# Crossbar transposes, a new decay path and regrouped gates in a fused gate-loop and GEGLU kernel

## The chip, the cores and the metric

The kernel runs on one core of one Trainium2 chip. The metric is device microseconds (us) of that core, the median of several executions. Before the change: 344.27 us, median of 3 runs (342.91 to 344.88). Ratios and verdicts use runs of the state "fast" alone; a median that includes slow runs is marked.

Engines are named as the profile names them: PE is TensorE (matmul), PEld its weight loads, DVE is VectorE, ACT is ScalarE, POOL is GpSimd, SP is SyncE. "SPq" and "ACTq" are the instruction queues of SyncE and ScalarE, which here issue DMAs.

## The reference, cut to what matters

A gated linear recurrence with a complex gate per element gives `y`; a GEGLU feed-forward with a gated residual follows.

```python
# q, k, v, a_re, a_im: (4, 8, 768, 48) float32
mag = np.sqrt(a_re * a_re + a_im * a_im)
scale = np.minimum(mag, 0.999) / (mag + 1e-06)
a = (a_re * scale) + 1j * (a_im * scale)          # written here as one complex number
for t in range(S):                                # state S_re, S_im: (B, H, D, D)
    S = a[:, :, t, :, None] * S
    S.real += einsum('bhd,bhe->bhde', k[:, :, t], v[:, :, t])
    y[:, :, t] = einsum('bhd,bhde->bhe', q[:, :, t], S.real)
# x: (3072, 384) from y;  weights 384x1536, 384x1536, 1536x384, 384x384
out = x + sigmoid(x @ w_res) * ((gelu(x @ w_gate) * (x @ w_val)) @ w_out)
```

The kernel turns the recurrence into chunks of 128 steps. The running product of the gates becomes a cumulative sum of logarithms and angles (`E`, `Ei`, `CS`), which is multiplied into q and k; then a chunk is an ordinary masked attention, plus a carried state `G` that is scaled by a decay `M` from one group to the next.

## The kernel before: the parts that matter

Twelve *groups* of two chunks each are worked on; two groups are a *unit*, so there are six units. ScalarE loads a table of functions at the start of each stage; these 18 loads mark the stages in the trace. Per unit there is a gate stage, first with the natural-log table (**NL**), then with the trigonometric table (**TRIG**), and a feed-forward phase with the **GELU** table, which also holds the products and the attention of the next unit's first group.

Pools (buffers) that the change touches:

```python
lda = ctx.enter_context(tc.tile_pool(name="lda", bufs=6))     # a_re, a_im of a group
ldq = ctx.enter_context(tc.tile_pool(name="ldq", bufs=4))     # q, k of a group
pE  = ctx.enter_context(tc.tile_pool(name="pE", bufs=2))      # E, Ei and fg (angles)
psT = ctx.enter_context(tc.tile_pool(name="psT", bufs=1, space=PSUM))
```

The products `Q` and `K` are transposed on PE, four heads at a time, and copied out by ScalarE and VectorE; the scores `at` follow:

```python
tp = psT.tile([128, 1024], BF, tag="tp", name="tp")
for j in range(4):
    nc.tensor.transpose(out=tp[0:DD, j * 128:j * 128 + 128], in_=Q(x), identity=ident)
# ... the same for K
nc.scalar.copy(out=qk[0:DD, 0:512], in_=tp[0:DD, 0:512])
nc.vector.tensor_copy(out=qk[0:DD, 512:1024], in_=tp[0:DD, 512:1024])
for j in range(4):
    nc.tensor.matmul(out=at[:, j], lhsT=qk[...K...], rhs=qk[...Q...], start=True, stop=True)
```

The decay `M` needs rows turned into columns; this is done through DRAM, on GpSimd's queue, in two separate trips (`m1`: the raw row, sent while the *previous* stage runs; `m2`: rows of `E` and `Ei`). The products that make `M` are on VectorE at 0.95 of the gate stage:

```python
def decay0(g): turn("m1", g, [T["lm", g][0:1, 0:DM]])
def decay2(g): turn("m2", g, [T["E", g - 1][127:128, DM:W], T["Ei", g][0:1, 0:DM]])
def decay3(g):      # M = m2[0] * m2[1] * exp(m1), on VectorE
    ...
weave((0.0, 0.12, csls), (0.05, 0.5, ...p1...), (0.01, 0.01, dec1), (0.12, 0.45, exs),
      (0.46, 0.46, dec), (0.2, 0.65, cst), (0.7, 0.95, atn + sin), (0.95, 0.95, dec3), ...)
```

`weave` sorts steps by a fraction of the phase, which sets the order in the program; a scheduler then sets each engine's order. In the feed-forward phase: `weave((0.0, 1.0, gv), (0.0, 0.4, pr), (0.3, 0.95, att_steps(u + 1, 0)))`, where `gv` are the gate/up steps, `pr` the products Q and K, and the attention steps have high priority. The attention also holds `G = (dk + G) * M`.

Of the kernel before, what the change touches and what calls it, by code (L numbers as in the profile page):

```python
# [28 lines left out]
def kernel(  # L29
# [24 lines left out]
    NU = NG // 2  # L54
    MAGIC = 12582912.0
# [32 lines left out]
    lda = ctx.enter_context(tc.tile_pool(name="lda", bufs=6))  # L88
    ldq = ctx.enter_context(tc.tile_pool(name="ldq", bufs=4))
    ldv = ctx.enter_context(tc.tile_pool(name="ldv", bufs=6))  # L90
    pS = ctx.enter_context(tc.tile_pool(name="pS", bufs=2))
    pE = ctx.enter_context(tc.tile_pool(name="pE", bufs=2))
    pQ = ctx.enter_context(tc.tile_pool(name="pQ", bufs=2))
    pK = ctx.enter_context(tc.tile_pool(name="pK", bufs=1))
    sqp = ctx.enter_context(tc.tile_pool(name="sqp", bufs=2))
# [8 lines left out]
    psT = ctx.enter_context(tc.tile_pool(name="psT", bufs=1, space=PSUM))  # L104
    psA = ctx.enter_context(tc.tile_pool(name="psA", bufs=1, space=PSUM))
    psY = ctx.enter_context(tc.tile_pool(name="psY", bufs=1, space=PSUM))
    psD = ctx.enter_context(tc.tile_pool(name="psD", bufs=1, space=PSUM))

# [25 lines left out]
    def load_q(g):  # L134
        for nm, src in (("q", q), ("k", k)):
            t = ldq.tile([128, C, H, D], FP, tag=nm, name=nm)
            for c in range(C):
                nc.sync.dma_start(out=t[:, c], in_=rows(src, g, c))
            T[nm, g] = t
        t = ldv.tile([128, C, H, D], BF, tag="v", name="v")  # L140
        for c in range(C):
            nc.gpsimd.dma_start(out=t[:, c], in_=rows(v, g, c))  # L142
        T["v", g] = t
# [76 lines left out]
    def cs_t(g, c):  # L220
        s = g % NS
        th = T["th", g]
        if c == 0:
            T["fg", g] = pE.tile([128, C * H, 2, D], FP, tag="fg", name="fg")
        sl = slice(c * DM, (c + 1) * DM)
        cs = psM.tile([128, DM], FP, tag="mm", padded_shape=[128, 512], name="cst")
        nc.tensor.matmul(out=cs, lhsT=tmat[c], rhs=th[:, sl], start=True, stop=(s == 0))  # L227
        if s > 0:
            nc.tensor.matmul(out=cs, lhsT=ones2pi, rhs=T["P", g], start=False, stop=True)
        cs3 = cs.rearrange("p (h d) -> p h d", h=H)  # L230
        fg = T["fg", g]
        hs = slice(c * H, (c + 1) * H)
        r = pS.tile([128, H, D], FP, tag="r", name="r")
        nc.vector.tensor_scalar(out=r, in0=cs3, scalar1=MAGIC, scalar2=MAGIC, op0=OP.add, op1=OP.subtract)  # L234
        nc.vector.tensor_tensor(out=fg[:, hs, 1, :], in0=cs3, in1=r, op=OP.subtract)
        if c == C - 1:
            nc.vector.scalar_tensor_tensor(out=fg[:, :, 0, :], in0=fg[:, :, 1, :], scalar=-1.0, in1=fg[:, :, 1, :],  # L237
                                           op0=OP.mult, op1=OP.max)
# [10 lines left out]
    def turn(nm, g, srcs):  # L249
        n = len(srcs)  # L250
        md = dr.tile([n, DM], FP, tag="d" + nm, name="d" + nm)
        for i, src in enumerate(srcs):
            nc.gpsimd.dma_start(out=md[i:i + 1, :], in_=src)
        m = mp.tile([128, n, H], FP, tag=nm, name=nm)
        for u in range(2):
            nc.gpsimd.dma_start(out=m[u * D:(u + 1) * D].rearrange("p r h -> p (r h)"),
                                in_=md.rearrange("r (h d) -> d (r h)", h=H))
        T[nm, g] = m

    def decay0(g):  # L260
        turn("m1", g, [T["lm", g][0:1, 0:DM]])

    def decay1(g):
        m = T["m1", g]
        act(out=m[0:DD], in_=m[0:DD], func=AF.Exp)

    def decay2(g):
        turn("m2", g, [T["E", g - 1][127:128, DM:W], T["Ei", g][0:1, 0:DM]])

    def decay3(g):  # L270
        m = T["m2", g]
        M = mp.tile([128, H], FP, tag="M", name="M")
        nc.vector.tensor_tensor(out=M[0:DD], in0=m[0:DD, 0], in1=m[0:DD, 1], op=OP.mult)
        nc.vector.tensor_tensor(out=M[0:DD], in0=M[0:DD], in1=T["m1", g][0:DD, 0], op=OP.mult)
        T["M", g] = M

    def products(g):
        def x0():
            qE = pK.tile([128, W], BF, tag="qE", name="qE")
            nc.vector.tensor_tensor(out=qE, in0=flat(T["q", g]), in1=T["E", g], op=OP.mult)  # L280
            T["qE", g] = qE

        def x1():
            kE = pK.tile([128, W], BF, tag="kE", name="kE")
            nc.vector.tensor_tensor(out=kE, in0=flat(T["k", g]), in1=T["Ei", g], op=OP.mult)
            T["kE", g] = kE

        def mk(nm, src):
            def x():
                t = pQ.tile([128, C * H, 2, D], BF, tag=nm, name=nm)  # L290
                sb = T[src, g].rearrange("p (x u d) -> p x u d", u=1, d=D).to_broadcast([128, C * H, 2, D])
                nc.vector.tensor_tensor(out=t, in0=T["CS", g], in1=sb, op=OP.mult)  # L292
                T[nm, g] = t
            return x
        return [x0, mk("Q", "qE"), x1, mk("K", "kE")]


    def attention(g, c):
# [4 lines left out]
        def Q(x):  # L303
            return T["Q", g][:, x].rearrange("p u d -> p (u d)")

        def K(x):
            return T["K", g][:, x].rearrange("p u d -> p (u d)")

        def V(h):
            return T["v", g][:, c, h]  # L310

        def grp(hg):
            def a():
                tp = psT.tile([128, 1024], BF, tag="tp", name="tp")
                for j in range(4):
                    x = c * H + hg * 4 + j
                    nc.tensor.transpose(out=tp[0:DD, j * 128:j * 128 + 128], in_=Q(x), identity=ident)  # L317
                for j in range(4):
                    x = c * H + hg * 4 + j
                    nc.tensor.transpose(out=tp[0:DD, 512 + j * 128:640 + j * 128], in_=K(x), identity=ident)  # L320
                qk = sqp.tile([128, 1024], BF, tag="qk", name="qk")
                nc.scalar.copy(out=qk[0:DD, 0:512], in_=tp[0:DD, 0:512])  # L322
                nc.vector.tensor_copy(out=qk[0:DD, 512:1024], in_=tp[0:DD, 512:1024])  # L323
                st["qk", hg] = qk
                at = psA.tile([128, 4, 128], FP, tag="at", name="at")
                for j in range(4):
                    nc.tensor.matmul(out=at[:, j], lhsT=qk[0:DD, 512 + j * 128:640 + j * 128],  # L327
                                     rhs=qk[0:DD, j * 128:j * 128 + 128], start=True, stop=True)
                atm = sqp.tile([128, 4, 128], BF, tag="atm", name="atm")
                nc.vector.tensor_tensor(out=atm, in0=at, in1=mask4, op=OP.mult)  # L330
                st["atm", hg] = atm
            return a
# [17 lines left out]
        def dk():  # L350
# [5 lines left out]
            for h in range(H):  # L356
                nc.tensor.matmul(out=d[0:DD, h * D:(h + 1) * D], lhsT=K(c * H + h), rhs=V(h),  # L357
                                 start=(c == 0 and h == 0), stop=(h == H - 1), skip_group_check=True)

        def yy():  # L360
            y = psY.tile([128, DM], FP, tag="y", padded_shape=[128, 512], name="y")
            for h in range(H):
# [3 lines left out]
                if not first:  # L366
                    nc.tensor.matmul(out=ys, lhsT=st["qk", hg][0:DD, j * 128:j * 128 + 128],  # L367
# [62 lines left out]
    def op_step(u, jj):  # L430
# [9 lines left out]
        nc.sync.dma_start(out=out[t0:t0 + 128, :], in_=ot)  # L440
# [27 lines left out]
    def phase_x(u):  # L468
# [4 lines left out]
        d2 = [g for g in g2 if g % NS > 0]  # L473
# [11 lines left out]

        def p1(g):
            return p1_steps(g) + ([call(decay0, g)] if g % NS > 0 else [])
        csls = [call(csl, g, c) for g in g1 for c in range(C)]
        exs = [ex for _ in g1 for _ in range(C)]
        dec = [call(decay2, g) for g in d1]  # L490
        atn = [table("trig_and_small")] + [call(p1_arctan, g) for g in g2]
        cst = [call(carry, g) for g in g1] + [call(cs_t, g, c) for g in g1 for c in range(C)]
        sin = [call(p2_sin, g) for g in g1]
        dec1 = [call(decay1, g) for g in d1]
        dec3 = [call(decay3, g) for g in d1]
        table("natural_log_exp_and_others")()
        if u < 0:

            for f in [st for g in g1 for st in p1(g)] + csls + exs + dec + zip_steps([p1(g) for g in g2]) + dec1:
                f()  # L500
            for f in atn[:1] + [call(p1_arctan, g) for g in g1] + cst + sin + atn[1:] + dec3:
                f()
            return
        weave((0.0, 0.12, csls), (0.05, 0.5, zip_steps([p1(g) for g in g2])), (0.01, 0.01, dec1), (0.12, 0.45, exs),
              (0.46, 0.46, dec), (0.2, 0.65, cst), (0.7, 0.95, atn + sin), (0.95, 0.95, dec3), (0.0, 0.8, att), (0.1, 1.0, ops))

# [10 lines left out]
    for g in gs(0) + gs(1):  # L517
        load_a(g)
    for g in gs(0):
        load_q(g)  # L520
    after_landing(T["k", 0], load_w_in)
    for u in range(-1, NU + 1):
        phase_x(u)
        for g in gs(u + 3):
            load_a(g)
        if u == -1:
            for g in gs(1):
                load_q(g)
            after_landing(T["k", 2], load_w_out)
        phase_y(u)  # L530
        for g in gs(u + 3):
            load_q(g)

# [29 lines left out]
```

## Time and profile before

| | before |
|---|---|
| median us | 344.27 |
| span of the profiled run, us | 341.4 |
| mean granted clock of PE | 0.93 |
| PE / DVE / ACT busy, us | 267.3 / 245.4 / 203.0 |
| DMA traffic, MB | 30.25 |

The page of the profile of the kernel before: busy microseconds and share of the span by engine; then the span in 40 slices (tenths busy; granted clock of PE; DMA engines); then the chain of waits that ended last, by engine and by line.

```profile
span 341.4 us, 5552 instructions
PE 267.3 (78%) x2054; PEld 160.6 (47%) x2080; DVE 245.4 (72%) x440; ACT 203.0 (59%) x338; POOL 67.1 (20%) x104
...
PE   0330544298689979899897999779999989999995
...
PEclk9996585559699999999999999999999999999999
DMA  9999999999999999527422620021000210002002
...
PE 47%; DMA 18%; DVE 15%; ACT 9%; issue 7%; POOL 3%; ACTq 0%; DVEq 0%; POOLq 0%
```

The DMA engines are full for 16 slices (137 us). In the first eight of these (68 us) PE is busy for 5 tenths at most, at a granted clock that falls to 0.5; after that PE is at 6 to 9 tenths until the last slice. PE has the largest part of the chain (47%). The windows view of two units in the steady part (window, its length, busy time and count of instructions by engine, granted clock, DMA share, GB/s):

```profile
140.80:187.20 46.40, 41.72 (x345) 24.84 (x347) 39.35 (x71) 33.40 (x56) 8.64 (x12) 1.00 0.37 52
187.20:234.50 47.30, 42.27 (x346) 25.50 (x348) 40.49 (x73) 33.84 (x57) 6.04 (x10) 1.00 0.22 43
```

A unit takes 46.4 and 47.3 us, of which PE is busy 42, DVE 40, ACT 33.5. Taking work from PE should shorten a unit, until DVE or a latency is next. That was the idea of the change.

### The profile page before, as it was taken

The page shows a single profiled execution, that of the slowest core. Times are in us where ns is not written, and L with a number is a line of the kernel's source. Part 1 is how long each engine was busy: PE and PEld are TensorE (multiplying, and loading weights), DVE is VectorE, ACT ScalarE, POOL GpSimd, SP SyncE. Part 2 cuts the span into 40 slices and gives each one's busy share as a digit, 9 for nine tenths or more (in the row PEclk, how much of TensorE's full clock was granted, in tenths as well). Part 3 has the DMA queues.
Part 4 walks back from the last instruction along what each step waited for, and adds up shares of the span by engine and source line. Part 5 has one row for each costly group of instructions (what it writes and reads, how often), then busy time and mean ns, then how long its engine had stood idle before and what let it go on. Part 6 is the DMA issues. An engine that isn't in the chain of part 4 may idle for free.

```text
span 341.4 us, 5552 instructions
## 1 busy us (share of the span) xinstructions
PE 267.3 (78%) x2054; PEld 160.6 (47%) x2080; DVE 245.4 (72%) x440; ACT 203.0 (59%) x338; POOL 67.1 (20%) x104
## 2 busy tenths in 40 slices
PE   0330544298689979899897999779999989999995
PEld 0110224275256545465554566445665556565452
DVE  1322696249999649999389998499994799855443
ACT  3365434349665696756896656977568275662530
POOL 9423710050522224102232000150001300000000
PEclk9996585559699999999999999999999999999999
DMA  9999999999999999527422620021000210002002
GB/s 139 136 139 175 176 184 196 175 170 171 155 167 162 169 133 172 109 46 72 25 63 54 118 46 2 2 48 47 3 2 1 50 46 2 0 2 92 2 1 92
DMA packets 135258, 30.25 MB, mean 89 GB/s; under 512 B 127168, under 2 KB 135232, under 8 KB 135232
## 3 DMA queue, kind: packets, MB, share of 16 engines
q1 hardware_dynamic: 103296, 23.60, 40.6%
q0 software_dynamic: 31936, 6.31, 21.9%
q8 instruction: 16, 0.26, 0.3%
q14 instruction: 10, 0.08, 0.1%
HBM read 31.33 MB, written 4.76 MB: 106 GB/s over the span
## 4 chain that ended last, share of the span: by engine, by line
PE 47%; DMA 18%; DVE 15%; ACT 9%; issue 7%; POOL 3%; ACTq 0%; DVEq 0%; POOLq 0%
PE vp L414 12%; PE gp L410 11%; PE op L434 6%; DMA dm_266<-ar 4%; DMA v<-in_v_dram 4%; PE tp L320 3%; PE at L327 3%; PE tp L317 3%; PE rp L426 3%; DMA dm_663<-Ei 2%; ACT L445 2%; DVE fg L237 2%; DVE r L234 2%; DMA dm_219<-ar 2%; ACT CS L119 2%
## 5 line engine op out<-in xcount | busy, mean ns | idle before, releaser
L410 PE MATMUL gp<-xT,wg 128*128 128x512 bf16 x196 | 61.5, 382 | 7.6 <-DVE xT L401 4.6
L414 PE MATMUL vp<-xT,wv 128*128 128x512 bf16 x210 | 60.3, 382 | 0.3
L322 ACT COPY qk<-tp 96x512 bf16<-96x512 bf16 x48 | 27.9, 581 | 28.3 <-PE tp L320 15.1
L180 DVE TENSOR_TENSOR ai<-s,ai 128x768 f32<-128x768 f32 x12 | 11.1, 955 | 38.5 <-ACT s L119 26.9
L330 DVE TENSOR_TENSOR atm<-at,mask_81 128x512 bf16<-128x512 f32 x48 | 32.8, 683 | 7.2 <-PE at L327 7.2
L410 PEld LDWEIGHTS <-wg 128*128 128x128 bf16 x216 | 20.0, 98 | 23.0 <-issue 8.9
L317 PE MATMUL tp<-ident,Q 128*96 128x128 bf16 x192 | 20.1, 231 | 13.4 <-DVE qk L323 8.6
L142 POOL DMA_DIRECT2D v<-in_v_dram x24 | 21.3, 902 | 43.0 <-PE y L367 22.4
L414 PEld LDWEIGHTS <-wv 128*128 128x128 bf16 x216 | 20.4, 98 | 19.3 <-issue 0.8
L317 PEld LDWEIGHTS <-Q 128*96 128x96 bf16 x192 | 17.3, 131 | 21.4 <-issue 10.0
L323 DVE COPY qk<-tp 96x512 bf16<-96x512 bf16 x48 | 19.9, 414 | 10.1 <-ACT qk L322 9.6
L203 PE MATMUL csl<-ar,lt0a 128*128 128x384 f32 x24 | 12.3, 601 | 18.6 <-DVE ar L189 18.5
L119 ACT ACTIVATE CS<-fg,hpi 128x768 bf16<-128x768 f32 x12 | 11.2, 935 | 24.1 <-DVE fg L237 24.1
L445 ACT ACT_TABLE_LOAD x18 | 23.1, 1283 | 1.0 <-PEq L547 0.7
L320 PE MATMUL tp<-ident,K 128*96 128x128 bf16 x192 | 22.1, 235 | 0.0
L227 PE MATMUL cst<-ai,lt0b 128*128 128x384 f32 x24 | 11.6, 568 | 13.4 <-ACT ai L119 13.1
L327 PE MATMUL at<-qk 96*128 96x128 bf16 x192 | 20.4, 228 | 0.1
L437 DVE SCALAR_TENSOR_TENSOR ot<-sg,op 128x384 f32<-128x384 f32 x24 | 13.2, 549 | 9.4 <-PE op L434 9.4
L365 PE MATMUL y<-v,atm 128*128 128x48 bf16 x192 | 17.9, 187 | 2.5 <-DVE atm L330 2.4
L365 PEld LDWEIGHTS <-atm 128*128 128x128 bf16 x192 | 13.5, 98 | 12.8 <-DVE atm L330 11.6
L320 PEld LDWEIGHTS <-K 128*96 128x96 bf16 x192 | 17.3, 133 | 0.0
L357 PEld LDWEIGHTS <-K 128*96 128x96 bf16 x160 | 13.3, 138 | 6.5 <-DVE K L292 4.2
(155 smaller groups left out, 626.3 us busy)
## 6 DMA issues: line engine op xcount, KB each, us to landing
ar<-in_a_re_dram SPq DMA_DIRECT2D x24, 192.0 KB, 5.7
ai<-in_a_im_dram SPq DMA_DIRECT2D x24, 192.0 KB, 5.5
q<-in_q_dram SPq DMA_DIRECT2D x24, 192.0 KB, 5.1
k<-in_k_dram SPq DMA_DIRECT2D x24, 192.0 KB, 5.0
out_dram<-ot SPq DMA_DIRECT2D x24, 192.0 KB, 1.9
v<-in_v_dram POOLq DMA_DIRECT2D x24, 96.0 KB, 6.3
wg<-in_moe_w_gate_dram POOLq DMA_DIRECT2D x4, 288.0 KB, 9.2
wv<-in_moe_w_val_dram POOLq DMA_DIRECT2D x4, 288.0 KB, 10.5
```

The costliest lines, as they stand in the source:

```text
L142: nc.gpsimd.dma_start(out=t[:, c], in_=rows(v, g, c))
L317: nc.tensor.transpose(out=tp[0:DD, j * 128:j * 128 + 128], in_=Q(x), identity=ident)
L320: nc.tensor.transpose(out=tp[0:DD, 512 + j * 128:640 + j * 128], in_=K(x), identity=ident)
L322: nc.scalar.copy(out=qk[0:DD, 0:512], in_=tp[0:DD, 0:512])
L323: nc.vector.tensor_copy(out=qk[0:DD, 512:1024], in_=tp[0:DD, 512:1024])
L327: nc.tensor.matmul(out=at[:, j], lhsT=qk[0:DD, 512 + j * 128:640 + j * 128], rhs=qk[0:DD, j * 128:j * 128 + 128], start=True, stop=True)
L330: nc.vector.tensor_tensor(out=atm, in0=at, in1=mask4, op=OP.mult)
L365: nc.tensor.matmul(out=ys, lhsT=st["atm", hg][:, j], rhs=V(h), start=True, stop=first)
L410: nc.tensor.matmul(out=gp, lhsT=wg[:, fi, ffi * 128:(ffi + 1) * 128], rhs=xT[:, fi, :], start=(fi == 0), stop=(fi == KD - 1))
L414: nc.tensor.matmul(out=vp, lhsT=wv[:, fi, ffi * 128:(ffi + 1) * 128], rhs=xT[:, fi, :], start=(fi == 0), stop=(fi == KD - 1))
L434: nc.tensor.matmul(out=ps, lhsT=h2[:, ffi, jj * 128:(jj + 1) * 128], rhs=wo[:, ffi, :], start=(ffi == 0), stop=(ffi == KF - 1))
L445: tab(nc.scalar.preload_act_table_set(nm))
```

## The change

Its intent: take the transposes of Q and K off PE, and their copies off ScalarE and VectorE, by letting the DMA crossbar do them (from group 2 on); take the decay trips out from behind the weights on GpSimd's queue, by giving them ScalarE's queue; and start unit 0 early, by doing the gates of unit 0 alone, then of unit 1 alone, then of units 2 and 3 in one table phase. The crossbar's output needs room in SBUF, so buffers are given up elsewhere: `a` 6 to 5, `q`/`k` 4 to 3, `fg` 2 to 1. Stores move to GpSimd, because SyncE now issues the transposes.

```diff
-    lda = ctx.enter_context(tc.tile_pool(name="lda", bufs=6))
-    ldq = ctx.enter_context(tc.tile_pool(name="ldq", bufs=4))
+    lda = ctx.enter_context(tc.tile_pool(name="lda", bufs=5))
+    ldq = ctx.enter_context(tc.tile_pool(name="ldq", bufs=3))
+    pF = ctx.enter_context(tc.tile_pool(name="pF", bufs=1))       # fg, two buffers before
+    pT = ctx.enter_context(tc.tile_pool(name="pT", bufs=3))       # QT, KT
+    Qb = [singles.tile([128, C * H, 128], BF, name="Qb%d" % i) for i in range(2)]   # padded to 128; Kb alike
...
+    def decay_rows(g):                                            # all three rows in one trip
+        er = pS.tile([1, DM], FP, tag="r", name="er")
+        act(out=er, in_=T["lm", g][0:1, 0:DM], func=AF.Exp)
+        md = dr.tile([3, DM], FP, tag="md", name="md")
+        for i, src in enumerate((T["E", g - 1][127:128, DM:W], T["Ei", g][0:1, 0:DM], er)):
+            nc.scalar.dma_start(out=md[i:i + 1, :], in_=src)
...
+    def decay(g):                                                 # fetch m (nc.scalar.dma_start), then M
+        nc.gpsimd.tensor_tensor(out=M[0:DD], in0=m[0:DD, 0], in1=m[0:DD, 1], op=OP.mult)
+        nc.gpsimd.tensor_tensor(out=M[0:DD], in0=M[0:DD], in1=m[0:DD, 2], op=OP.mult)
...
+                if g >= PE_TURNED:                                # PE_TURNED = 2
+                    for c in range(C):
+                        tt = pT.tile([128, H, 128], BF, tag=nm + "T", name=nm + "T")
+                        nc.sync.dma_start_transpose(out=tt, in_=t[:, c * H:(c + 1) * H].rearrange("p x e -> p (x e)"))
...
-        nc.sync.dma_start(out=out[t0:t0 + 128, :], in_=ot)
+        nc.gpsimd.dma_start(out=out[t0:t0 + 128, :], in_=ot)
...
+        new = g1 if u == 0 else g1 + g2 if u == 1 else g2          # which groups' gates in which stage
...
-    for g in gs(0) + gs(1):
+    for g in gs(0):
         load_a(g)
     for g in gs(0):
         load_q(g)
-    after_landing(T["k", 0], load_w_in)
+        load_v(g)
+    for g in gs(1):
+        load_a(g)
+    after_landing(T["ar", 2], load_w_in)
+    for g in gs(1):
+        load_q(g)
```

(Cut: the transposes on PE that stay for groups 0 and 1, the new weave of the gate stages, the order of the loads after this. Also in the edit: the PSUM pool `psT` is gone, these transposes use the shared pool `psM`, and the pool of the scores, `psA`, has two buffers instead of one.)

## The prediction

> **What bounds the kernel now.** Two regimes (windows view, 40-slice page). Until about 121 us the DMA engines are the floor: 9 tenths busy in slices 1 to 17 (145 us), PE only 3 to 5 tenths until 68 us at a granted clock of 0.50 to 0.82. The chain of waits there holds decay round trips on the GpSimd queue, behind weights and v: dm_266<-ar 13.9 us, m_268 4.6 us, dm_663 8.4 us; ScalarE waits 8.9 us for m_268. The first gate/up matmuls of unit 0 come at 96 us, the GELU table of unit 1 at 140.8 us. From there a unit of two groups takes 46 us; between 167.1 and 213.8 us (46.7 us) PE is busy 42.1, DVE 39.7, ACT 33.7 us: PE first, DVE close behind, DMA a third or less.
>
> **What the change removes.** In that unit: PE transposes of Q and K 3.1 + 3.4 us, ScalarE copies L322 4.7 us, DVE copies L323 3.3 us, and 0.3 us of decay products moved to GpSimd (groups 2 to 11 only). PE falls to about 35.6 us, DVE to 36.1, ACT to 29. As PE bounds and DVE is next, I expect 5 us (4 to 6) off a unit: 41 us, about 21 us over the 4.3 units after 141 us. The last 38 us (feed-forward of the last unit) stay.
>
> **What it adds.** 40 crossbar transposes of 256 KB on the SyncE queue, 8 a unit. The Trainium skill, "DMA: Bandwidth & Descriptors", latency table, gives 261 GB/s for a transpose: by that an estimate of 1.0 us each, plus issue and landing; I expect 1.5 to 3 us on the queue, 12 to 24 us of a unit, and about 4 us from K to KT landing. No trace of before shows one. PE has about 4 us of other work between K and the scores, so a stall of 1 to 2 us a unit.
>
> **The start.** Decay waits behind weights vanish (ScalarE's own ring). Unit 0 should start its feed-forward at 60 to 70 us instead of 96. But SyncE issues in order: 53 loads stand before the first transpose (q of group 5 even waits for the products of group 2: three q buffers). In before the 52nd load issued at 97 us, so unit 1's first scores wait until 92 to 97 us and PE stalls 20 to 30 us in the middle of unit 0's feed-forward. Then the third gate stage does units 2 and 3 together: 8 more activations of 0.84 us, 21 us become about 29. So unit 1's GELU table comes at 130 to 145 us, against 140.8: most of the early gain is given back.
>
> **Sum.** 344 - 21 (steady) - 5 (start) - 3 (last unit, decay) = 315 us. Range 292 to 338.
>
> **What would show each step.** (a) PE busy falls by about 35 us in all, ACT by 23, DVE by 16; (b) GELU table to GELU table 41 us in the later units; (c) transposes 1.5 to 3 us apart on the queue, DMA share up in the second half; (d) ScalarE's and GpSimd's waits for m and dm gone; (e) first gate/up matmuls at 60 to 70 us; (f) PE waiting for a DMA (QT, KT) once for over 15 us near 70 to 95 us; (g) third gate stage about 29 us.
>
> **What would make it wrong.** Transposes over 5 us each: SyncE's queue becomes the bound (350 us); (f) not happening (295 us); DVE or latencies keeping the unit at 46 us (330 us); ScalarE waiting for the md rows to land in each gate stage (+2 us a unit).
>
> Chances: faster by over 2% 0.87, within 2% 0.08, slower 0.05.

## The result, and the profile after

The kernel after took 372.05 us, median of 4 runs (368.52 to 373.88); before, in the same rounds, 343.59 us. The ratio is 1.081 (95% interval 1.072 to 1.091): **8% slower**, where 8% faster had been predicted, and far outside the range of 292 to 338. (Ratios here are the mean time of one kernel's fast runs over that of the other's of the same rounds, so not quite the ratio of the medians that are quoted. Executions over 1.5% slower than the fastest of the same kernel are left out of the means.)

The page of the kernel after, same lines:

```profile
span 369.9 us, 4849 instructions
PE 268.0 (72%) x1738; PEld 150.9 (41%) x1760; DVE 233.1 (63%) x384; ACT 185.8 (50%) x298; POOL 51.0 (14%) x93
...
PE   0356377106595929597998779985799987999993
...
PEclk9988555757568976798999989999989998999998
DMA  9999999989899403949955589043851127612002
...
PE 28%; issue 21%; DMA 19%; DVE 13%; ACT 9%; SPq 5%; POOL 2%; ACTq 1%; POOLq 0%; DVEq 0%
```

The instructions did go: 316 fewer on PE, 12.3 us less on DVE, 17.2 us less on ACT. But PE's busy time did not fall (267.3 to 268.0). Two things meet here. The transposes overlap with other matmuls in PE's pipeline: a run below that leaves them out at a granted clock of 0.946 (z2) has 247.2 us, only 20.1 less, where the sum of their single durations had promised 35. And the mean granted clock fell from 0.93 to 0.867: a gate matmul took 402 ns in the mean instead of 382. The Trainium skill, "TensorE: Matmul & The Clock Gate", section "What's actually happening", says that the clock is halved after an idle window of some 3.4 us; this trace agrees in part: in the hole from 74.0 to 80.3 us, without one matmul, the granted clock is 0.50, and it is 0.66 in the 9.7 us after; but it is also 0.50 from 46 to 56 us, where PE is busy for 7.9 of 10 us. PE's share of the chain fell from 47% to 28%. It waits more.

The starts of the table loads, read from ScalarE's timeline, show where (us from the start of the span; the length of the stage up to the next start in brackets):

| stage | before | after |
|---|---|---|
| TRIG of unit 0's gates | 35.3 | 23.2 |
| NL, 2nd stage | 54.1 (30.7) | 36.6 (43.8) |
| TRIG, 2nd stage | 84.9 (9.2) | 80.3 (19.5) |
| GELU, unit 0 | 94.0 (26.0) | 99.9 (30.1) |
| NL, 3rd gate stage | 120.0 (10.5) | 130.0 (21.2) |
| TRIG | 130.5 (10.3) | 151.1 (16.1) |
| GELU, unit 1 | 140.8 (26.4) | 167.3 (24.8) |
| GELU, unit 2 | 187.2 | 214.0 |
| GELU, unit 3 | 234.5 | 259.4 |
| GELU, unit 4 | 278.6 | 304.1 |
| GELU, unit 5 | 304.5 | 331.1 |
| end | 341.4 | 369.9 |

The whole loss is there when unit 1's GELU table comes: 26.5 of 28.5 us. After it a unit takes 46.8, 45.3 and 44.7 us (before 46.4, 47.3, 44.0): the 5 us a unit that had been promised are not there either. Windows of the kernel after: a hole in the start, then two units.

```profile
65.50:80.30 14.80, 1.15 (x20) 0.76 (x20) 1.29 (x2) 0.00 (x0) 1.75 (x2) 0.65 1.33 150
...
167.25:214.00 46.75, 39.57 (x280) 22.30 (x284) 36.52 (x61) 29.84 (x48) 6.90 (x10) 0.96 0.74 122
214.00:259.40 45.40, 38.35 (x275) 21.89 (x280) 36.76 (x62) 29.76 (x50) 2.03 (x5) 0.96 0.55 99
```

Two waits were plain in the trace. **First**, ScalarE is idle from 65.5 to 80.3 us. The timeline of the kernel after (start, length, what, in brackets the idle time of the engine before it and what ended it):

```profile
73.55 4.56 SPq L147 DMA_DIRECT2D q<-in_q_dram  x2
77.88 0.24 ACTq L265 DMA_DIRECT2D md<-Ei  x1
...
80.09 0.22 ACTq L265 DMA_DIRECT2D md<-er  x1
80.34 1.28 ACT L450 ACT_TABLE_LOAD   x1 [14.89 <-DMA ai<-in_a_im_dram]
```

ScalarE had to issue the decay rows before its next table load, and the issue waited for *loads of SyncE*. The built instruction lists show why: with few exceptions each DMA on SyncE's or ScalarE's queue first waits for the DMA eight before it, through one of eight completion counters that the two queues share in this program. So two decay DMAs of 1.5 KB waited in turn behind loads, the last of them of `a_im`. The Trainium skill, "DMA: Bandwidth & Descriptors", section "Issuing engines are not separate DMA queues", says that DMAs of different issuing engines run on the same 16 DMA engines. This trace agrees (its DMA view puts the queues of SyncE, GpSimd and ScalarE at 46.1, 22.6 and 2.9% of the same 16 engines) and adds that the issuing engine itself can be held.

**Second**, PE waits for the transposes. The view of the tile KT in the kernel after (count; duration of the issue in ns, min/median/max; then what the idle time of PE and of its weight loads, which overlap, ended with before KT was used, us and times), and the chain around unit 0's attention (start, length, what):

```profile
L299 SPq DMA_TRANSPOSE KT<-Kb_154 x10: 1260/1308/2690, 100.1 to 308.8; - x10
L299 SPq DMA_TRANSPOSE KT<-Kb_155 x10: 1231/1438/3245, 111.0 to 321.4; - x10
...
  DMA KT<-Kb_155: 12.8, 7
  DMA KT<-Kb_154: 11.5, 7
```

```profile
100.09 3.34 DMA KT<-Kb_154
...
111.04 7.05 DMA KT<-Kb_155
```

The queue takes a transpose every 1.3 us, but in the chain KT lands 3.3 to 7 us after its issue, and PE stands idle for a part of that time.

How much each of these and the other parts of the change is worth, the trace cannot say, because waits overlap. That was the task of the experiments.

### The profile page after: what moved, and what is told of

It reads as the page before. It is cut to its first block, busy times and chain, and to the rows that moved or that the text cites. A ratio compares the mean times of both kernels' runs of the same rounds, so it can differ in the third digit from the quotient of the medians.

```text
span 369.9 us, 4849 instructions
## 1 busy us (share of the span) xinstructions
PE 268.0 (72%) x1738; PEld 150.9 (41%) x1760; DVE 233.1 (63%) x384; ACT 185.8 (50%) x298; POOL 51.0 (14%) x93
## 3 DMA queue, kind: packets, MB, share of 16 engines
q1 hardware_dynamic: 142080, 29.37, 46.1%
q0 software_dynamic: 31680, 10.92, 22.6%
## 4 chain that ended last, share of the span: by engine, by line
PE 28%; issue 21%; DMA 19%; DVE 13%; ACT 9%; SPq 5%; POOL 2%; ACTq 1%; POOLq 0%; DVEq 0%
PE vp L419 6%; PE gp L415 6%; DMA m<-md 5%; SPq L140 5%; DMA ai<-in_a_im_dram 5%; DMA KT<-Kb_155 4%; PE at L332 3%; PE csl L214 3%; ACT L450 2%; DMA KT<-Kb_154 2%; DVE ar L199 2%; PE cst L238 2%; DVE fg L248 2%; PE rp L431 2%; ACT s L128 2%
## 5 line engine op out<-in xcount | busy, mean ns | idle before, releaser
L419 PE MATMUL vp<-xT,wv 128*128 128x512 bf16 x205 | 64.1, 404 | 0.7 <-issue 0.2
L445 POOL DMA_DIRECT2D out_dram<-ot x24 | 13.2, 548 | 182.6 <-DVE ot L443 182.6
L214 PE MATMUL csl<-ar,lt0a 128*128 128x384 f32 x24 | 14.4, 695 | 25.6 <-DVE ar L200 25.6
L332 PE MATMUL at<-QT,KT 96*128 96x128 bf16 x192 | 20.9, 246 | 16.3 <-DMA KT<-Kb_155 5.4
L450 ACT ACT_TABLE_LOAD x18 | 23.1, 1283 | 16.2 <-DMA ai<-in_a_im_dram 14.9
L419 PEld LDWEIGHTS <-wv 128*128 128x128 bf16 x216 | 20.9, 102 | 21.8 <-issue 3.9
L332 PEld LDWEIGHTS <-KT 96*128 96x128 bf16 x192 | 15.3, 111 | 23.9 <-DMA KT<-Kb_155 7.4
L375 ACT CAST x<-y 128x384 bf16<-128x384 f32 x24 | 11.5, 478 | 18.6 <-PE y L372 13.7
L128 ACT ACTIVATE sg<-rp 128x384 f32<-128x384 f32 x24 | 11.8, 490 | 14.5 <-PE rp L431 14.5
L370 PEld LDWEIGHTS <-atm 128*128 128x128 bf16 x192 | 14.9, 102 | 8.6 <-DVE atm L335 6.4
L226 DVE TENSOR_TENSOR P<-ai 128x384 f32<-128x384 f32 x8 | 4.3, 553 | 21.9 <-ACT ai L128 21.8
L281 DVE TENSOR_TENSOR qE<-q,E 128x768 bf16<-128x768 f32 x12 | 11.4, 953 | 9.6 <-ACT E L128 9.6
L214 PEld LDWEIGHTS csl<-ar,lt0a 128*128 128x128 f32 x24 | 5.4, 254 | 29.6 <-DVE ar L200 18.7
```

What stands on the lines that cost most here:

```text
L128: tab(nc.scalar.activation(**kw))
L214: nc.tensor.matmul(out=cs, lhsT=lmat[c], rhs=T["lm", g][:, sl], start=True, stop=True)
L332: nc.tensor.matmul(out=at[:, j], lhsT=KT[0:DD, hg * 4 + j], rhs=QT[0:DD, hg * 4 + j], start=True, stop=True)
L370: nc.tensor.matmul(out=ys, lhsT=st["atm", hg][:, j], rhs=V(h), start=True, stop=first)
L419: nc.tensor.matmul(out=vp, lhsT=wv[:, fi, ffi * 128:(ffi + 1) * 128], rhs=xT[:, fi, :], start=(fi == 0), stop=(fi == KD - 1))
L450: tab(nc.scalar.preload_act_table_set(nm))
```

## The experiments

Eighteen kernels ran, in five sets; the kernels of a set shared the runs of before. The theory at the start was that two new waits (ScalarE's queue; unit 1's late gates) ate what the crossbar gained; the rivals were the crossbar's own latency, and the buffers that had been given up.

### Undoing one part of the change

`a1_pe_all`: after, with the transposes of all groups back on PE (`PE_TURNED = NG`; they go through the shared PSUM pool).

```diff
-    PE_TURNED = 2
+    PE_TURNED = NG
```

> The kernel after, with all transposes on TensorE again (no crossbar). Start theory (the 28 us are lost before unit 1's GELU table at 167 us, to ScalarE's decay DMAs waiting on SyncE's loads and to the long third gate stage): stays at 365 to 375 us. Crossbar theory (late KT tiles, SyncE's queue and DMA contention are the cost): comes back to 345 us or below.

Measured: 380.06 us, 1.105 of before (1.099 to 1.110), outside both expectations. Putting the transposes back on PE does not mend the kernel after: it is 8 us slower still. That does not clear the crossbar, because these transposes share the pool `psM` and are not those of before; z1 below takes them away altogether.

`a2_decay_pool`: after, with the decay DMAs on GpSimd's queue.

```diff
-            nc.scalar.dma_start(out=md[i:i + 1, :], in_=src)
+            nc.gpsimd.dma_start(out=md[i:i + 1, :], in_=src)
   (and the fetch of m alike)
```

> The kernel after, with the decay rows' DMAs issued by GpSimd instead of ScalarE. Start theory: ScalarE's 12.4 us wait before md<-Ei and 2.2 us before md<-er go, unit 0's GELU table comes at about 86 us instead of 99.9, total about 358 us. Crossbar theory: within 3 us of the kernel after.

Measured: 368.35 us, 1.069 (1.064 to 1.074). The hole at 65.5 us is gone: the TRIG table comes at 62.7 us instead of 80.3. But unit 0's GELU table gains only 5.5 us of these 17.7 (94.4 instead of 99.9), and the total 3.7, where 14 had been expected. Behind the wait stood another: VectorE then waited for `er`, which shares its buffers with `r`, and for `M`.

`a3_gates_before` (gates and order of loads of before; crossbar and ScalarE's ring stay) and `a4_decay_gates` (both undone: what is left is crossbar, small buffers, stores, and the new decay on GpSimd). Their edit: the weave of the gate stages and the load loop are those of before.

```diff
-        new = g1 if u == 0 else g1 + g2 if u == 1 else g2
-        ... (three kinds of gate stage)
+        weave((0.0, 0.12, csls), (0.05, 0.5, p1), (0.12, 0.45, exs), (0.46, 0.46, dec), (0.2, 0.65, cst), ...)
```

> The kernel after, with the gate stages and the order of loads of the kernel before (one unit ahead from the beginning); crossbar and ScalarE's ring stay. Start theory: third gate stage back from 37 to about 21 us, total 350 to 358 us (the ScalarE waits for lanes may remain). Crossbar theory: 365 us or more.

> Both undone: decay DMAs on GpSimd and gate stages and load order of before; what is left of the change is the crossbar with its buffers, the stores on GpSimd and the exponential of the decay row taken before the DMA. Start theory: 333 to 345 us, at least level with before, since late units take about 1 us less each. Crossbar theory: 360 us.

Measured: 365.01 us, 1.061 (1.052 to 1.070), and 370.60 us, 1.075 (1.070 to 1.081). The start theory had 350 to 358 and 333 to 345 us for them. With the decay on ScalarE's queue, the new gate stages with their order of loads cost 7 us (372.05 against 365.01); with it on GpSimd's queue they do not cost anything (a2 368.35 against a4 370.60, in the same rounds). So the 7 us are not a cost of the gates by themselves. The third gate stage, 37.3 us in after, is 28.9 us in a3 (from 133.69 to 162.61 us). But no undoing of these brings the kernel near 344 us: with decay queue and gates both back, 27 us stay. So the theory that the start alone is to blame fell.

### Doing one part alone

Each kernel here is the kernel before with one part of the change.

`c1_stores`: `nc.gpsimd.dma_start` for the output. `c2_buffers`: the three smaller pools and nothing else. `c3_ring`: the new decay scheme on ScalarE's ring. `c4_crossbar`: crossbar, with the smaller pools and the stores on GpSimd.

```diff
 c2_buffers
-    lda = ctx.enter_context(tc.tile_pool(name="lda", bufs=6))
-    ldq = ctx.enter_context(tc.tile_pool(name="ldq", bufs=4))
+    lda = ctx.enter_context(tc.tile_pool(name="lda", bufs=5))
+    ldq = ctx.enter_context(tc.tile_pool(name="ldq", bufs=3))
+    pF = ctx.enter_context(tc.tile_pool(name="pF", bufs=1))     # fg
```

> The kernel before, with only its output stores moved from SyncE to GpSimd. Queue theory (stores on GpSimd stand in one in-order queue with the decay rows and v): 348 to 355 us, of which about 1.5 us at the very end, where the last store lands 4.4 us after its data instead of 2.7. Latency theory (the crossbar's KT tiles and nothing else): 344 to 346 us.

> The kernel before, with only the buffers that the change gives up: a 6 to 5, q and k 4 to 3, fg 2 to 1. Buffer theory (the second group's fg must wait for the first group's sines, loads wait for products): 350 to 362 us, 2 to 3 us more in each gate stage. Rival (buffers are idle slack): 343 to 346 us.

> The kernel before, with only the decay changed: exponential taken before the DMA, rows on ScalarE's ring, products on GpSimd. If the ring's waits for SyncE's loads are a cost by themselves: 352 to 360 us with ScalarE idle 10 us or more before a decay DMA while loads are busy. If the ring is the gain that it was meant to be: 330 to 340 us, as the 8.9 us wait for m goes.

> The kernel before with the crossbar, its smaller buffers and the stores on GpSimd; decay and gates as before. Latency theory: 350 us or more, with two waits of PE for KT of 2 to 4 us in each unit, and a unit no shorter than 46 us. If the crossbar is a gain that the gates and the ring gave away: 325 to 338 us.

Measured, beside 343.88 us of before in these rounds: c1 346.98 us, 1.009 (1.004 to 1.014); c2 359.70, 1.048 (1.042 to 1.055); c3 356.48, 1.036 (1.032 to 1.040); c4 372.28, 1.082 (1.078 to 1.086). Each of these parts alone costs time, c1 less than 2%. (The regrouped gates alone on the kernel before were not run.) Three of these had not been in the prediction as costs: the buffers, 16 us, the stores, 3 us, and the decay scheme, 13 us, which had been booked as a gain. And c4, the crossbar with its buffers and stores, is already as slow as the whole change.

### Which buffer

`e1_fg1`: before, with `fg` in one buffer and all else as it was. `d1_fg2`: after, with `fg` in two.

```diff
 e1_fg1 (on before)                        d1_fg2 (on after)
+    pF = ...(name="pF", bufs=1)           -    pF = ...(name="pF", bufs=1)
-    T["fg", g] = pE.tile(...)             +    pF = ...(name="pF", bufs=2)
+    T["fg", g] = pF.tile(...)
```

> The kernel before, with only fg 2 to 1 (a 6, q and k 4 stay). If fg makes up the cost of the smaller buffers: 355 to 360 us, nearly the 359.7 of all three together. If the a and q buffers do: 344 to 348 us.

> The kernel after, with the second fg buffer given back (a 5, q and k 3 as in the change). If fg is what the smaller buffers cost: 356 to 362 us, from the trig table to the GELU table 2.5 to 3 us less in each later gate stage (10.3 to 11.5 us becomes about 8). If the a and q buffers are: within 3 us of 372.

Measured: e1 357.54 us, 1.041 (1.037 to 1.046): nearly all of the 16 us come from the one buffer of `fg`. d1 366.98 us, 1.067 (1.062 to 1.072): given back to the kernel after, it brings 5 us only, which is between the two expectations. By the table loads all of e1's loss lies between TRIG and GELU of the gate stages: 15.0, 13.8, 12.3, 11.8 and 14.3 us in the second to sixth stage, against 9.2, 10.3, 9.7, 10.3 and 13.8 in before, together 13.9 us. The view of the tile fg, of before and then of e1 (us and times that engines sat idle until this ended):

```profile
  DVE fg L237: 24.1, 12
```

```profile
  DVE fg L238: 38.9, 11
  ACT CS L120: 2.0, 2
```

ScalarE's sines wait 24.1 us for `fg` in before and 38.9 us in e1. With one buffer the second group's `fg` may not be written until the first group's sines have read theirs. The wait for that itself is small (2.0 us). But the scheduler filled the gap in VectorE's order with the products of `M`, ahead of the rest of `fg`, and those wait for the decay trip. The view of the tile M, of before and then of e1:

```profile
  DMA m_247<-dm_244: 4.2, 1
  DMA m_3118<-dm_3115: 1.8, 1
  DMA m_666<-dm_663: 0.2, 1
```

```profile
  DMA m<-dm: 13.7, 5
```

VectorE waits 6.2 us for `m` in before and 13.7 in e1 (14.2 in c2). So about half of the 14 us is read from the trace as this wait, and the rest as the two groups no longer overlapping; no run separates the two.

### Mending the kernel after

`d2_er_own`: a2 with two buffers of its own for `er`. `d3_mended`: d2 with the gates and loads of before, two buffers of fg (`a` stays at 5, `q` at 3).

```diff
-        er = pS.tile([1, DM], FP, tag="r", name="er")
+        er = mp.tile([1, DM], FP, tag="er", name="er", bufs=2)
```

> The kernel after, with decay DMAs on GpSimd as in a2_decay_pool (368.4 us) and buffers of its own for the exponentiated decay row er, which shares the two buffers of the rounding tile r. If DVE's 11.1 us wait for md<-er at 68 to 79 us was on the path: about 10 us less than a2, 356 to 360 us, and unit 0's GELU table at 84 us. If another wait lies behind it (the wait for the M products): 364 to 368 us.

> The crossbar, with gate stages and loads of before, decay on GpSimd, own buffers for er, two fg buffers. If buffers, lanes and gates are the whole of the loss: 335 to 345 us. If the KT waits and the a and q buffers keep their part: 350 to 358 us.

Measured: d2 370.10 us, 1.078 (1.073 to 1.083), no gain over a2's 368.35, a miss of both theories. d3 368.42 us (median of four runs, one of them slow), 1.068 (1.059 to 1.076, fast runs), also outside both expectations. The waits say why d2 gained nothing. Of a2, and of d2 (engine, line, releaser; us in total, times, longest):

```profile
DVE r L245 <- DMA md<-er: 11.1, 1, 11.1
```

```profile
DVE G L349 <- POOL M L275: 17.1, 2, 15.6
```

VectorE no longer waits 11.1 us for the buffer of `er`, but its next instruction in order, `G`, waits 15.6 us for `M`: both stand at the end of the same trip of the decay rows through DRAM. Taking away the first of two waits for one thing buys nothing.

### What transposes cost if they are free

Two kernels give wrong results: the transposes of groups 2 to 11 are left out, and the scores read untransposed data of the same shape. `z1_free_after` on after (no crossbar DMA), `z2_free_before` on before (no PE transposes, no copies).

```diff
 z1_free_after
-                        nc.sync.dma_start_transpose(out=tt, in_=...)
-                QT, KT = T["QT", g, c], T["KT", g, c]
+                QT, KT = T["Q", g][:, c * H:(c + 1) * H], T["K", g][:, c * H:(c + 1) * H]     # for g >= 2
```

> The kernel after with no transpose at all for groups 2 to 11: the score matmuls read the untransposed tiles, so the result is wrong on purpose; shapes, counts and all else stay. It takes away the crossbar's queue time, traffic and the waits for KT and QT at once. If those waits are what the crossbar costs: 345 to 355 us, and a feed-forward phase (GELU table to next log table) of 23 to 24 us. If fg, lanes and gates are the whole loss: 365 us or more.

> The kernel before with the TensorE transposes and both copies of groups 2 to 11 left out in the same way (result wrong on purpose); all buffers as before. It is the most that any free transpose could bring: 35 us of PE, 23 of ACT, 17 of DVE. If PE bounds the later units as I predicted: 310 to 318 us. If the gate stages' chain of ScalarE and DVE bounds them, as the kernel after suggests: 325 to 335 us.

Measured: z1 352.87 us (median of four runs, two of them slow; the fast two took 347.90 and 352.43), 1.018 (1.008 to 1.028, fast runs); z2 324.68 us, 0.946 (0.940 to 0.952). So the prediction's largest term was near in size: PE transposes and their copies cost the kernel before 19 us (343.71 less 324.68; predicted 21). But z2 lies above the 310 to 318 us that its expectation had for PE as the bound, and next to the 325 to 335 of the rival. The windows view of z2, one unit:

```profile
136.40:179.30 42.90, 37.97 (x282) 21.34 (x285) 36.50 (x63) 29.35 (x49) 9.93 (x14) 1.00 0.42 60
```

42.9 us against 46.4 for the same unit in before. By the table loads the whole gain lies in the feed-forward phase (GELU to NL): that of unit 1 falls from 26.4 to 22.8 us, while the gate stage after it, which holds none of these transposes (79 matmul records in both), takes 20.1 us in both. In before PE is busy for 25.7 us of that phase and for 16.1 of that gate stage. So the unit's average, PE first and DVE close behind, mixes a phase that PE fills with one that it does not. And z1 says that the crossbar's DMAs cost the kernel after some 19 us in the profiled executions, both fast (spans of 369.9 and 350.7 us); the mean of two fast runs alone, of other rounds than after's, would make it some 22. What the crossbar saves, waiting for it takes back.

The table loads of z1 show where: the feed-forward phase (GELU to NL) of unit 0 is 30.1 us in after and 20.8 in z1, those of units 3 and 4 are 26.6 and 27.0 in after and 21.8 and 22.5 in z1; together 18.5 of the 19.2 us. Units 1 and 2 do not gain (24.8 and 24.0 us in after, 24.8 and 23.5 in z1), and from GELU to GELU they take 46.8 and 44.8 us even without any transposes. There other parts of the change hold the time: in c2, the smaller buffers alone, the same units take 51.1 and 48.2 us, where before takes 46.4 and 47.3.

### The decay scheme

`e2_er_pool`: before with the new decay scheme, on GpSimd's queue as before, and own buffers for `er`. `e4_m_late`: e2 with the two products of `M` written at 0.95 of the stage instead of 0.46.

```diff
 e4_m_late against e2_er_pool
         T["m", g] = m
+    def decay_products(g):
+        m = T["m", g]
         M = mp.tile([128, H], FP, tag="M", name="M")
...
-              (0.46, 0.46, dec), (0.2, 0.65, cst), (0.7, 0.95, atn + sin), ...
+              (0.46, 0.46, dec), (0.2, 0.65, cst), (0.7, 0.95, atn + sin), (0.95, 0.95, dec3), ...
```

> The kernel before with the decay row exponentiated before its DMA, all on GpSimd's queue with buffers of its own for er; stores stay on SyncE, transposes on TensorE. It differs from c3_ring (356.5 us) in the queue and in er's buffers. If ScalarE's waits for lanes held by SyncE's loads were c3's cost: 335 to 345 us. If the cost is in the decay scheme itself: 352 to 358 us.

> This is e2_er_pool (the kernel before with the new decay scheme on the GpSimd queue, 357.4 us) with one thing moved: the two products that make M are written at 0.95 of the gate stage, as in the kernel before, in place of 0.46, right behind the fetch of m. Theory A: the 13 us of the decay scheme come from where M and G stand in the order of GpSimd and VectorE, so that G, placed early, holds VectorE up while M is still on its way (8.6 us in the profile of e2): at most 348 us, and no wait of VectorE for M over 3 us. Rival B: they come from the later request alone (the third row of md is now made and sent at the end of the exponentials instead of a stage earlier, and m is fetched after it), wherever the products stand: 354 to 359 us. In between both have a part.

Measured: e2 357.36 us, 1.038 (1.034 to 1.043); e4 356.70 us, 1.037 (1.033 to 1.041). The scheme thus costs 13 us on either queue (c3 356.48), so that a ring of its own is not what it lacks (e2 also gives `er` buffers of its own). And writing the products of `M` later in the program changes nothing. By the numbers that is what rival B expected; but the other half of theory A's expectation, no wait of VectorE for M over 3 us, did not come about, so the run did not take away what it was to take away. The view of the tile G, of e2 and then of e4 (what its engine sat idle for, us and times):

```profile
  POOL M L264: 15.5, 4
```

```profile
  POOL M L268: 16.0, 4
```

The timeline of unit 1's gate stage shows how it comes about. Before, then e4:

```profile
139.72 0.16 DVE L273 TENSOR_TENSOR M<-m_1258 96x8 f32<-96x8 f32 x1
...
141.36 0.55 DVE L341 TENSOR_TENSOR G<-dk,M 96x384 f32<-96x384 f32 x1
```

```profile
133.44 0.49 POOL L254 DMA_DIRECT2D md<-er  x1 [2.08 <-ACT er L119]
...
144.03 0.19 POOL L267 TENSOR_TENSOR M<-m 96x8 f32<-96x8 f32 x1 [3.60 <-DMA m<-md]
144.31 0.20 POOL L268 TENSOR_TENSOR M<-M,m 96x8 f32<-96x8 f32 x1
144.54 0.55 DVE L335 TENSOR_TENSOR G<-dk,M 96x384 f32<-96x384 f32 x1 [5.34 <-POOL M L268]
```

In before, M is VectorE's own work, and the scheduler has put M and G behind the stage's last `fg` (138.1 us). In e4, M is on GpSimd, G stands in VectorE's order *before* the second group's `r` and `fg` (145.0 to 148.1 us), and the whole engine waits 5.3 us for a trip whose third rows were sent at 133.4 and 134.6 us. The sines of that stage, and with them the GELU table, come after that: TRIG to GELU is 15.7 us there, 10.3 in before.

A second thing can be read in e4's trace. `er` reads the buffer of `a_re` until the end of the exponentials, so the loads of `a_re` for the unit three later, which SyncE issued at 120.8 us in before, are issued at 133.2 to 138.5 us in e4, behind a load of q that itself waits from 114.7 to 130.2 us for a free buffer. Whether this costs anything no run tells. That the place of G costs most of the 13 us is argued from the lines above, not shown: no run moved G back in VectorE's order. How these parts share the 13 us stays open.

### The crossbar by itself, and the crossbar with something to hide its latency

`k3_crossbar_alone`: before with the crossbar and nothing else, but for one q/k buffer less, two buffers each of QT and KT to make it fit, and the PSUM pools of after. Stores stay on SyncE, fg keeps two buffers, the decay is that of before. `k1_crossbar_late`: k3 with the first group's attention later in the feed-forward phase and, from unit 1 on, without high priority.

```diff
 k1_crossbar_late against k3_crossbar_alone
-        weave((0.0, 1.0, gv), (0.0, 0.4, pr), (0.3, 0.95, att_steps(u + 1, 0)))
+        weave((0.0, 1.0, gv), (0.0, 0.4, pr), (0.5, 1.0, att_steps(u + 1, 0, u + 1 > 0)))
...
-        return [hi(f) for f in (enter, grp(0), dk, grp(1), yy)]
+        return [f if low else hi(f) for f in (enter, grp(0), dk, grp(1), yy)]
```

> The kernel before with nothing but the crossbar transposes (groups 2 on): one q/k buffer less to make room (4 to 3), two buffers each of KT and QT, stores still on SyncE, fg with two buffers, a with six, the old decay. c4_crossbar had the same with the small buffers and the stores on GpSimd: 372.3 us. Theory A (buffers and latencies of KT add up as in the ledger: free transposes -19, waits for KT and the queue +19): 341 to 350 us. Rival B (the crossbar costs more than it saves, whatever the buffers): 355 to 372 us. In the profile PE waits for KT or QT 1.5 to 5 us at a time, over 20 us in all.

> k3_crossbar_alone with the attention of a unit's first group written later in the feed-forward phase before it (0.5 to 1.0 instead of 0.3 to 0.95) and without high priority, so that about four more gate/up steps (some 8 us of PE) stand between the K product and the first scores that need KT. Theory A (what eats the crossbar's gain is the time from issue to landing of KT, and PE had nothing else placed before the scores): 325 to 338 us, at least 8 us under k3_crossbar_alone, the waits of PE for KT in the first group gone. Rival B (the gain is eaten by loads and transposes that queue up behind each other on SyncE): within 5 us of k3_crossbar_alone, the waits at other places.

Measured, beside 343.82 us of before: k3 351.77 us, 1.023 (1.017 to 1.028); **k1 331.86 us, 0.965 (0.961 to 0.969)**. k3 lies just over the 341 to 350 us of its theory A, and far under the 372 us of c4: without the small `fg` and `a` pools and the moved stores the crossbar costs 8 us instead of 28. k1 is where its theory A put it, 20 us under k3. It gives the right result, and it is faster than both kernels of this study: 3.5% under before, 11% under after (331.86 over 372.05, of other rounds).

The view of the tile KT, of k3 and of k1 (issues on the queue; idle time of PE and of its weight loads before KT is used; landing):

```profile
L304 SPq DMA_TRANSPOSE KT<-Kb x20: 1231/1314/3227, 101.5 to 303.4; - x20
...
  DMA KT<-Kb: 50.7, 20
...
DMA to landing us min/median/max: 3.0/3.3/6.8
```

```profile
L304 SPq DMA_TRANSPOSE KT<-Kb x20: 1232/1282/1704, 100.8 to 287.4; - x20
...
  DMA QT<-Qb: 6.2, 4
  DMA KT<-Kb: 3.4, 2
...
DMA to landing us min/median/max: 3.0/3.2/3.9
```

The same 20 transposes of KT at the same rate, landing after the same 3.2 to 3.3 us in the median; in k3 that time is waited for (50.7 us over PE and its weight loads, which overlap), in k1 it is not (3.4 us). The engines' orders in the built kernels agree: in k1 eight whole gate/up steps of PE stand in front of a unit's first scores, in k3 three to seven, mostly four. But in k3 half of the wait (25.2 of the 50.7 us) is in unit 0's feed-forward phase, and there it is not landing alone: K is ready at 92.1 us, and SyncE issues its first transpose at 101.5 us, behind loads that stand before it in the queue. The first line of the chain of waits, of k3 and of k1:

```profile
PE 31%; DMA 19%; SPq 18%; DVE 15%; ACT 10%; issue 5%; POOL 1%; DVEq 0%; ACTq 0%
```

```profile
PE 34%; DMA 19%; DVE 17%; issue 15%; ACT 11%; SPq 2%; POOL 1%; POOLq 0%; DVEq 0%; ACTq 0%
```

and the windows view of k1, one unit, beside the 46.4 us of before and the 46.75 us of after:

```profile
142.60:185.70 43.10, 38.65 (x283) 21.38 (x284) 38.02 (x67) 29.41 (x49) 9.52 (x14) 1.00 0.74 114
```

In all, k1 is 12 us under before, where free transposes alone (z2) were 19 under it. From unit 1's GELU table to unit 5's, k1 takes 147.3 us and z2 148.9, so little of the crossbar's cost is left there; most of the 7 us between them is in unit 0's feed-forward phase (29.1 us against 21.6 in z2; 38.6 in k3). k1 changed two things at once, the place and the priority of the attention; which did more is not told apart. And a rival stands untested: no run moves the attention in a kernel without the crossbar. The feed-forward phases of units 1 to 4 are shorter in k1 (20.7 to 21.2 us) than with free transposes (21.9 to 22.9), so the move has some effect of its own, and part of the 20 us may be that.

### The sum

Single parts on the kernel before, in us over (or under) it:

| part | run | us |
|---|---|---|
| free transposes | z2 | −19.0 |
| crossbar alone (and q/k 4 to 3) | k3 | +8.0 |
| crossbar, attention later and low | k1 | −12.0 |
| a, q/k and fg buffers | c2 | +15.8 |
| of which fg alone | e1 | +14.0 |
| decay scheme, ScalarE's ring | c3 | +12.6 |
| decay scheme, GpSimd's queue | e2 | +13.7 |
| stores on GpSimd | c1 | +3.1 |
| crossbar, buffers, stores | c4 | +28.4 |
| whole change | after | +28.5 |

Crossbar, buffers and stores add up well (8.0 + 15.8 + 3.1 = 26.9, measured 28.4). The decay scheme and the gates do not add: on top of c4 they bring nothing (372.28 to 372.05), though the first costs 13 us alone and the second costs 7 within the kernel after (and nothing there once the decay is on GpSimd's queue, a2 and a4). One reason can be read from the traces above: c2, e1, e2, e4 and d2 all show VectorE held at the decay trip (13.7 to 17.1 us), and an engine waits for one trip once, whichever part of the change put the waiting step first. That is a reading, not a test; which part hides which was not taken apart.

## Why the prediction was wrong, point by point

Three steps failed: the room for the crossbar's output was counted as free (15.8 us by c2), the new decay path was booked as a gain (it costs 12.6 us, c3), and the stall of PE for KT was put at 1 to 2 us a unit (the crossbar costs the kernel after 19 us, z1). In c4 the crossbar, the buffers and the stores make up the whole loss; how the decay and the gates come to nothing on top of it stays open.

- **What bounds the kernel** was near in size: free transposes are worth 19 us (z2), where 21 was predicted, and 42.9 us a unit where 41 was. But "PE first" describes the feed-forward phase (PE busy for 25.7 of 26.4 us), not the gate stage (16.1 of 20.1), and z2 missed the 310 to 318 us that its expectation had for PE as the bound.
- **"about 4 us from K to KT landing ... so a stall of 1 to 2 us a unit"**: the latency was well guessed (3.3 us in the median in k3, up to 7), the stall was not. The prediction set "about 4 us of other work between K and the scores" against it and took the difference once for a unit; but each of a unit's two groups has two KT and two QT tiles, and the attention is of high priority, so PE comes to it early. Against z1 the crossbar costs 19 us in all, 9.3 of them in unit 0's feed-forward phase, 4.8 and 4.5 in those of units 3 and 4. Between k3 and z2 the phases of units 2 to 4 differ by 2.5 to 2.9 us each, not far from the prediction; those of units 0 and 1 by 17.0 and 5.6 us. That k1, with more work placed in between, is 20 us under k3, at the same rate of transposes on the queue, speaks for the time from K to the landed KT as the cost; in unit 0 the loads ahead on SyncE's queue are a part of that time. This is a mis-sized term.
- **The buffers given up were not costed** ("three q buffers" comes up at the start alone). That is the largest omission: 15.8 us by c2, 14.0 of them by `fg` going from two buffers to one (e1). The diff showed it in one line. These buffers are also what keeps units 1 and 2 of (b) at 46.8 and 45.3 us instead of 41: in z1 the units stay long without transposes, in c2 they become longer by the buffers alone. The pairing of the two is a reading; no run of the kernel after had all buffers of before.
- **"Decay waits behind weights vanish"** and (d): the wait only changed its form. ScalarE, which issues the decay rows now, was held for 14.9 us by loads of SyncE; and the scheme, with all three rows in one trip that starts when the last row is ready, costs 13 us by itself on either queue (c3, e2), where 5 us of gain for the start and part of 3 us for the last unit and decay had been booked.
- **(e) unit 0's feed-forward at 60 to 70 us**: it came at 99.9 us, later than before (94.0).
- **(f) PE waiting over 15 us for QT or KT near 70 to 95 us** did not happen as such: the first transpose was issued at 97.3 us, behind 57 loads (predicted: 53, and 92 to 97 us), but unit 0 was late too, and PE's long wait (65.5 to 80.3 us) was for ScalarE.
- **(g) third gate stage about 29 us**: 37.3 us (21.2 before its TRIG table, 16.1 after). The eight activations were counted, not that gates of two units make each of the two table phases a longer chain of ACT and DVE steps.
- **(a) PE busy −35, ACT −23, DVE −16**: +0.7, −17.2, −12.3. The instructions went. The 35 us were a sum of durations that overlap (z2: −20.1 us), and PE's clock was granted less (0.867), beside more idle time.
- **(c) transposes 1.5 to 3 us apart**: 1.3 us, slightly better, and the DMA share did go up. The estimate from the skill's bandwidth (1.0 us) was near; what mattered was the time to land.
- The stores' move was not costed: 3.1 us (c1). With the store on GpSimd the last store is issued 4.4 us before the end, with SyncE 2.7 us (365.5 to 369.9 and 338.7 to 341.4).
- "What would make it wrong" named DVE or latencies keeping the unit at 46 us, and put it at 330 us. The unit stayed at 46 us; but unit 1's GELU table came 26 us later than before, where that sum had the start earlier.

## What to carry to other kernels

Moving work from a busy engine to a DMA trades busy time for latency: here it paid only when other work of the waiting engine was *placed* in between. So try moving the consumer later in the same change (k3 to k1: 20 us for a few lines), and run the same move without the DMA beside it, which was not done here. What a change takes away to make room, such as a second buffer between two engines, is a term of the sum like any other, and here one buffer cost 14 us. When a wait is removed, look at what the next instruction of the same engine waits for before booking the gain: it may be the same thing.

## What the Trainium skill lacked or had wrong

- "Advanced Engine Details and Errata", section "X-Bar Transpose (TRN2)", says "TRN2 transpose DMAs are as fast as regular DMAs", and "DMA: Bandwidth & Descriptors", section "Latency and other measured facts", gives 261 GB/s in one kernel. The queue here takes 256 KB every 1.3 us, about 200 GB/s, which is somewhat less; no run compares a transpose with a regular DMA of the same data. And neither page gives the time from issue to landing of such a transpose within SBUF, beyond the second's general fit for a DMA of any kind: 3.0 us at least, 3.2 to 3.3 us in the median, up to 6.8 us beside loads (k3, k1). For a consumer that stands right behind, that is the figure that counts.
- "DMA: Bandwidth & Descriptors", section "Issuing engines are not separate DMA queues", says that issuing from several engines saves only the time on the sequencer. It lacks that an issuing engine can also *lose* time: in this program SyncE's and ScalarE's DMAs share eight completion counters, and ScalarE, with computing to do, was held 14.9 us by loads of SyncE.
- None of these pages has a duration for a row-to-column turn through DRAM (rows out, columns in). In e4 it took 9.4 us from the last row's issue (134.59 us) to the start of the products that need it (144.03 us), and VectorE waited 15.5 to 17.1 us a run for such trips (e2, e4, d2).
